# ScalarE issues the stores of its own results; the first batch is rotated at once, and the conversion of the first weights starts eight slots ahead of the first tile

## The chip, the cores and the metric

The kernel runs on one core of one Trainium2 chip. The metric is the device time of one execution in microseconds (us). Three timed runs of the kernel before gave 1304.89, 1307.54 and 1314.07 us; their median is 1307.54 us.

## What is computed

Three operators follow each other. Attention with rotated queries and keys (4 batches, 8 heads, 576 tokens, head size 64), then two layers of a feed-forward block over 2304 tokens of width 512 with an inner width of 2048. All inputs and outputs are float32 in the reference; the weights arrive as 64-bit floats.

```python
q_rot, k_rot = (rotate(q), rotate(k))       # x1*cos - x2*sin, x1*sin + x2*cos
scores = scale * np.matmul(q_rot, k_rot.transpose(0, 1, 3, 2))
attn = np.exp(scores - max); attn = attn / (sum + 1e-9)
x = np.matmul(attn, v)                      # then [B*S, H*D] = [2304, 512]
r = np.maximum(x @ w_in1, 0.0);  x = (s * r * r + b) @ w_out1
h = x @ w_in2;  out = (h / (1 + np.exp(-1.702 * h))) @ w_out2
```

## The kernel before, in words

**Attention.** The 8 heads of a batch are handled as 4 pairs. A *tile* is 128 query rows against 576 keys, and every tile has a number, its *slot*: 36 slots a batch, 144 in all. A pair has a first unit of 4 tiles (`k` = 0) and a second unit of 5; the first units of all four pairs come first (slots 0 to 15 of batch 0), then the second units. One tile is `score_tile` (TensorE makes `s`, VectorE takes the minimum and copies to `P`, ScalarE takes the exponential), `norm_tile` (GpSimd scales `P`), `turn_tile` (TensorE turns `P` into `t`, ScalarE and in the first 20 slots TensorE and ScalarE again split it into two float16 halves in `pt`), and at the end of a unit `weighted` (TensorE makes `av`, ScalarE scales it into `pt`, a store writes it to `xT` in DRAM).

**Rotation.** Before a pair can be scored, its q and its k are each loaded (`nat`), rotated by four elementwise instructions on GpSimd or VectorE (`rope_cross` twice, `rope_mul`, `rope_add`), turned by TensorE in two groups through one PSUM buffer (`r`), split by ScalarE and VectorE into two parts `z`, stored to DRAM (`ksp`, `qsp`) and loaded back (`k`, `qb`) by `fetch_pair`. In batch 0, VectorE rotates the q of pairs 0 and 1 (RV = 2) and GpSimd the other six. `plan_rope` starts pair p at slot -16 + 4p.

**Weights.** The 16 weight blocks `f` of each layer come in two *halves* (`m` = 0, 1) of 128x512. A half is loaded as 64-bit words (`stage`, 512 KB) and made into two float32 parts: one ScalarE scaling (L398), three VectorE instructions on the words (L399, L400, L403), one ScalarE copy (L406) and one GpSimd subtraction (L407). Layer 1's 32 halves are converted ahead of and among the tiles of batch 0: `CONV = (-12, 1.0)` puts block f at slot -12 + f. Eleven blocks are held in SBUF (`w0` to `w10`), five are written back to DRAM (`wd`) and streamed.

**Feed-forward layers.** `experts` makes *passes* over the tokens; a pass makes `l` (first product) and `acc` (second product) for all 16 blocks. From slot 22 of batch 0 on, its steps are put between the tiles. The first pass loads its `xl` from `xT` and thus needs the first units of all four pairs. After the last tile the passes run alone.

**Order of work.** The order on TensorE is pinned to the order in which the program is written. The other engines' queues are ordered by a scheduler from priorities (the slot) and its own estimate of when each instruction is ready. All DMAs are issued by SyncE in one queue (SP); each takes one of eight completion counters in turn (in the rows of order: DMAHW0 to DMAHW7) and waits first until the transfer that last used that counter has landed.

The lines printed here touch `rope_load`, `rope_cross` and `plan_rope` (rotation), `make_half` and `weight` (conversion), and `weighted` and `finish` (stores).

## Time and profile before

| what | value |
|---|---|
| median of three timed runs | 1307.54 us |
| the profiled execution, its own time | 1307.66 us |
| its span, first to last instruction | 1305.9 us |
| PE busy | 1119.6 us (86%) |
| DVE busy | 746.5 us (57%) |
| ACT busy | 676.7 us (52%) |
| POOL busy | 354.8 us (27%) |
| DMA | 202.5 MB, mean 155 GB/s |
| mean granted TensorE clock | 0.966 |

PE is TensorE, PEld its weight load, DVE VectorE, ACT ScalarE, POOL GpSimd, SP the queue of SyncE. Shares are averages over stretches with different limits: in its second half TensorE is busy nearly all the time, while in the first 200 us it is mostly idle and the other engines, the DMAs and the waits between them set the pace. So the profile is to be read by stretch.

### The profile page before, as it was taken

What the parts mean: (1) busy time and instruction counts of PE and PEld (TensorE: products, weight loads), DVE (VectorE), ACT (ScalarE), POOL (GpSimd) and SP (SyncE); (2) the same over time, 40 slices, a digit from 0 to 9 for tenths busy, and PEclk for the clock granted to TensorE, in tenths of its full rate; (3) what the DMA queues carried; (4) which work ended last, traced back from release to release, by engine and by line L of the source; (5) the groups of instructions that cost most, each with busy time, mean ns of one, the idle gap of its engine ahead of it and who ended that gap; (6) DMA issues with size and microseconds to landing.
All of it is one profiled execution on the core that took longest, in us unless ns stands there. A gap on an engine that the chain in (4) does not pass through costs nothing.

```text
span 1305.9 us, 21075 instructions
## 1 busy us (share of the span) xinstructions
PE 1119.6 (86%) x7432; PEld 991.4 (76%) x7432; DVE 746.5 (57%) x1652; ACT 676.7 (52%) x1483; POOL 354.8 (27%) x350
## 2 busy tenths in 40 slices
PE   0126568989989989999999996998999999999998
PEld 0024448988889888899889996876788888888887
DVE  7887735667657666757656657866633223232222
ACT  3347555666656666666656655665533223232232
POOL 5675743334324441444111112323100000000000
PEclk9998588999999999999999997999999999999999
DMA  7987765468756677665665528545303012021020
GB/s 241 307 272 243 243 173 149 139 196 252 224 155 211 197 230 228 191 212 169 187 195 172 166 73 289 166 148 170 117 17 113 1 49 81 17 74 24 17 81 17
DMA packets 131561, 202.50 MB, mean 155 GB/s; under 512 B 32512, under 2 KB 93440, under 8 KB 131456
## 3 DMA queue, kind: packets, MB, share of 16 engines
q1 hardware_dynamic: 131456, 201.15, 49.4%
q8 instruction: 59, 0.97, 0.3%
q14 instruction: 46, 0.38, 0.1%
HBM read 155.49 MB, written 45.61 MB: 154 GB/s over the span
## 4 chain that ended last, share of the span: by engine, by line
PE 56%; DMA 14%; DVE 9%; issue 8%; ACT 5%; POOL 4%; SPq 2%; DVEq 0%; POOLq 0%; ACTq 0%
PE acc L88 21%; PE l L88 21%; PE t L88 5%; PE s L88 4%; PE av L88 4%; DMA stage<-in_moe_w_in_dram 2%; DMA xT<-pt 2%; DVE P L299 2%; POOL w L407 2%; DMA xl<-xT 2%; DMA stage<-in_moe_w_out_dram 2%; DMA vr<-in_v_dram 1%; ACT P L308 1%; DVE stage L403 1%; DVE pt L342 1%
## 5 line engine op out<-in xcount | busy, mean ns | idle before, releaser
L88 PE MATMUL l<-xh,w 128*128 128x256 f32 (+1 forms) x1280 | 330.0, 331 | 11.9 <-ACT r L527 6.8
L88 PEld LDWEIGHTS l<-xh,w 128*128 128x128 f32 x1280 | 225.0, 191 | 36.0 <-ACT r L527 8.0
L88 PE MATMUL l<-xl,w 128*128 128x256 f32 (+1 forms) x640 | 211.8, 331 | 1.6 <-DVE xl L492 0.9
L319 POOL TENSOR_SCALAR P<-P,st 128x576 f32<-128x576 f32 x144 | 114.1, 793 | 345.3 <-DVE st L318 241.5
L88 PE MATMUL acc<-w,g 128*128 128x512 f32 x696 | 169.0, 392 | 4.9 <-ACT y L568 4.9
L308 ACT ACTIVATE P<-P,st 128x576 f32<-128x576 f32 x144 | 112.0, 778 | 101.8 <-DVE P L299 101.8
L532 DVE SCALAR_TENSOR_TENSOR r<-r,l 128x256 f32<-128x256 f32 x144 | 60.1, 417 | 180.2 <-ACT r L531 180.2
L88 PEld LDWEIGHTS acc<-w,g 128*128 128x128 f32 x696 | 131.1, 189 | 33.0 <-ACT y L568 5.8
L88 PE MATMUL t<-ident,P 128*128 128x128 f32 x720 | 111.7, 289 | 45.2 <-ACT pt L357 29.4
L531 ACT ACTIVATE r<-l 128x256 f32<-128x256 f32 x144 | 55.1, 383 | 178.9 <-PE l L88 178.8
L299 DVE TENSOR_SCALAR_CACHE_REDUCE P<-s 128x576 f32<-128x576 f32 x144 | 108.6, 754 | 62.9 <-PE s L88 57.4
L407 POOL TENSOR_TENSOR w<-stage,w 128x512 fp32r<-128x512 f32 x64 | 93.2, 1461 | 188.3 <-ACT w L406 146.2
L88 PEld LDWEIGHTS l<-xl,w 128*128 128x128 f32 x640 | 122.1, 191 | 13.3 <-DVE xl L492 2.0
L88 PEld LDWEIGHTS t<-ident,P 128*128 128x128 f32 x720 | 86.1, 148 | 58.7 <-issue 23.3
L88 PE MATMUL acc<-gh,w 128*128 128x256 f32 x616 | 129.4, 293 | 0.0
L88 PE MATMUL s<-k,qb 128*128 128x288 f32 x640 | 124.9, 324 | 3.9 <-DVE P L299 3.9
L342 DVE TENSOR_TENSOR pt<-t,pt 128x640 f16<-128x640 f32 x124 | 102.0, 822 | 28.3 <-ACT pt L340 27.6
L340 ACT CAST pt<-t 128x640 f16<-128x640 f32 x144 | 99.1, 688 | 21.2 <-PE t L88 19.4
L536 DVE TENSOR_TENSOR g<-r,g 128x256 fp32r<-128x256 f32 x160 | 71.0, 448 | 64.7 <-ACT g L535 64.7
L88 PEld LDWEIGHTS s<-k,qb 128*128 128x128 f32 x640 | 98.6, 204 | 12.2 <-issue 6.3
L529 ACT ACTIVATE r<-r,sb 128x256 f32<-128x256 f32 x144 | 86.1, 604 | 37.2 <-DVE r L528 36.7
L88 PEld LDWEIGHTS acc<-gh,w 128*128 128x128 f32 x616 | 102.6, 194 | 0.5 <-issue 0.4
(88 smaller groups left out, 1955.5 us busy)
## 6 DMA issues: line engine op xcount, KB each, us to landing
ws<-wd SPq DMA_DIRECT2D x96, 512.0 KB, 4.3
k<-ksp SPq DMA_DIRECT2D x32, 576.0 KB, 5.8
stage<-in_moe_w_in_dram SPq DMA_DIRECT2D x32, 512.0 KB, 5.0
stage<-in_moe_w_out_dram SPq DMA_DIRECT2D x32, 512.0 KB, 5.0
wd<-w SPq DMA_DIRECT2D x14, 512.0 KB, 5.0
ksp<-z SPq DMA_DIRECT2D x32, 160.0 KB, 5.0
qsp<-z SPq DMA_DIRECT2D x32, 160.0 KB, 4.4
vsp<-vz SPq DMA_DIRECT2D x16, 320.0 KB, 4.5
```

Source lines behind the costliest of these rows:

```text
L88: pin(nc.tensor.matmul(*args, **kw))
L299: nc.vector.tensor_scalar(pr.rearrange("p (n s) -> p n s", n=2), ps[:, :, :HS], -Q_SCALE, None, op0=ALU.mult, op1=ALU.min, accum_out=st[:, ...
L308: nc.scalar.activation(pr, pr, AF.Exp, bias=st[:, 0:1], scale=-1.0, accum_out=st[:, 1:2])
L319: nc.gpsimd.tensor_scalar(pr, pr, st[:, 2:3], 1.0, op0=ALU.mult, op1=ALU.mult)
L340: nc.scalar.copy(hi, pc)
L342: nc.vector.tensor_tensor(lo, pc, hi, op=ALU.subtract)
L403: nc.vector.scalar_tensor_tensor(low, high, 3, low, op0=ALU.logical_shift_left, op1=ALU.bitwise_or)
L407: nc.gpsimd.tensor_tensor(lo, f32(low), f32(hi), op=ALU.subtract)
L529: nc.scalar.activation(r, r, AF.Identity, bias=sb[:, 1:2], scale=sb[:, 0:1])
L531: nc.scalar.activation(r, ps[:, cols], AF.Tanh, scale=0.851)
L532: nc.vector.scalar_tensor_tensor(r, r, 1.0, ps[:, cols], op0=ALU.add, op1=ALU.mult)
L536: nc.vector.tensor_tensor(gl[:, cols], r, f32(gh[:, cols]), op=ALU.subtract)
```

## The change

Three things change. **Stores:** the stores of `xT`, of `x2` (between the layers) and of the output, 77 in all, are issued by ScalarE's queue instead of SP. **Rotation of batch 0:** loads and rotations of the four pairs start one slot apart (-16 + p instead of -16 + 4p), in buffers borrowed from weights `w5` to `w8` (`boot`), the turns are put at slots 4p - 7 and 4p - 8 and the ones after; VectorE also takes the q of pair 2 (RV = 3). **Conversion of layer 1:** block f is put at slot -8 + 1.5 f instead of -12 + f, its last two instructions (`split`, the ScalarE copy and the GpSimd subtraction) one slot later, and the raw words of blocks 0 to 12 go into the buffers of weights `w9` and `w10` instead of the ring of four that they shared with `xl`. `ACT_SHIFT` is empty, so that branch never runs.

```diff
+    boot = {}
+    BOOT = (5, 6, 7, 8)
 ...
     def rope_load(b, p, which, st):
-        nat = att.tile([128, RT, 2, HD], F32, tag="nat", name=f"nat{b}{p}{which}")
+        if b == 0:
+            if p not in boot:
+                boot[p] = wpool.tile([128, 2048], F32, tag=f"w{BOOT[p]}", name=f"boot{p}")
+            nat = boot_part(p, which)
+        else:
+            nat = att.tile([128, RT, 2, HD], F32, tag="nat", name=f"nat{b}{p}{which}")
 ...
     def weighted(g):
-        nc.sync.dma_start(
+        nc.scalar.dma_start(
             xT[128 * p : 128 * p + 128, b * S + q0 : b * S + q0 + T], xo[:, :T]
         )
 ...
     def make_half(t, w_in, w_out, f, m, nm):
+        elif f < HELD[0][-2]:
+            if m == 0:
+                stages[0] = wpool.tile(
+                    [128, 2, 512], U64, tag=f"w{len(HELD[0]) - 1 - f % 2}", name=f"stage{nm}"
+                )
+            raw = stages[0][:, m]
 ...
-        make_half(t, *W[layer], f, m, f"{layer}_{f}")
+        split = make_half(t, *W[layer], f, m, f"{layer}_{f}")
+        if layer == 0:
+            at(int(CONV[0] + CONV[1] * f) + WLAG, split)
+        else:
+            split()
 ...
     def finish(n, banks):
-                nc.sync.dma_start(
+                nc.scalar.dma_start(
                     x2[rows, t0 : t0 + T].rearrange("(c p) t -> p c t", p=128),
 ...
-                    nc.sync.dma_start(
+                    nc.scalar.dma_start(
                         ov[g // RT, ORDER_T[g % RT]], y[(j % 2) * 64 : (j % 2) * 64 + 64, j // 2]
 ...
-        gap = 2 if b else 1
         for g in range(2):
-            at(s + 4 + gap * g, rope_turn, b, p, which, g, st)
+            at(s + 4 + 2 * g if b else 4 * p + RT0 - which + g, rope_turn, b, p, which, g, st)
 ...
-    CONV = (-12, 1.0)
+    CONV = (-8, 1.5)
+    RT0 = -7
+    ACT_SHIFT = ()
+    WLAG = 1
-    RV = 2
+    RV = 3
 ...
-                eng = nc.vector if b == 0 and p < RV and which == 0 else nc.gpsimd
-                r = bounds[b - 1] + RS + 9 * p if b else -RL + 4 * p
+                eng = nc.vector if b == 0 and (p < RV and which == 0) else nc.gpsimd
+                r = bounds[b - 1] + RS + 9 * p if b else -RL + p
```

What this does to the queues is shown at three places. The first is GpSimd's queue from its first real work on, before the change (`rot` and `nat` are a rotation of the pair in the name's second digit, `w0_` the last step of a conversion, `vr` a memset in a value buffer).

```order
L195 TENSOR_TENSOR rot001_116<-nat001_112,tab_90 128x9x32 x2
L200 TENSOR_TENSOR nat001_112<-nat001_112,tab_90 128x576
L203 TENSOR_TENSOR nat001_112<-nat001_112,rot001_116 128x576
L407 TENSOR_TENSOR w0_0_128<-stage0_00_129,w0_0_128 128x512
L407 TENSOR_TENSOR w0_0_128<-stage0_01_137,w0_0_128 128x512
L407 TENSOR_TENSOR w0_1_158<-stage0_10_159,w0_1_158 128x512
```

The same place after the change (`boot0` to `boot3` are pairs 0 to 3, `nat101` is the k of batch 1).

```order
L208 TENSOR_TENSOR boot0_112<-boot0_112,tab_90 128x9x32 x2
L208 TENSOR_TENSOR boot1_115<-boot1_115,tab_90 128x9x32 x2
L213 TENSOR_TENSOR boot0_112<-boot0_112,tab_90 128x576
L213 TENSOR_TENSOR boot1_115<-boot1_115,tab_90 128x576
L208 TENSOR_TENSOR boot2_122<-boot2_122,tab_90 128x9x32 x2
L208 TENSOR_TENSOR boot3_134<-boot3_134,tab_90 128x9x32 x2
L216 TENSOR_TENSOR boot0_112<-boot0_112 128x576
L216 TENSOR_TENSOR boot1_115<-boot1_115 128x576
L208 TENSOR_TENSOR rot030_161<-boot3_134,tab_90 128x9x32 x2
L213 TENSOR_TENSOR boot2_122<-boot2_122,tab_90 128x576
L213 TENSOR_TENSOR boot3_134<-boot3_134,tab_90 128x576
L431 TENSOR_TENSOR w0_0_172<-stage0_0_173,w0_0_172 128x512
```

Pair 0's k was GpSimd's third instruction line and is now its seventh, behind half rotations of the three other pairs; the rotations of pairs 2 and 3 and of batch 1's first pair stand ahead of the first tile and not among the first sixteen any more.

The second place is VectorE's queue around the last part of q of pair 0 (`z000`), without which no tile can be scored; before the change:

```order
L403 SCALAR_TENSOR_TENSOR stage0_11_167<-stage0_11_167 128x512
L399 TENSOR_SCALAR stage0_20_200<-stage0_20_200 128x512
L217 TENSOR_TENSOR z000_188<-r0000_183,z000_188 128x2x256
L400 SCALAR_TENSOR_TENSOR stage0_20_200<-stage0_20_200 128x512
L403 SCALAR_TENSOR_TENSOR stage0_20_200<-stage0_20_200 128x512
L217 TENSOR_TENSOR z000_188<-r0001_219,z000_188 64x2x64
```

The same place after (`stage0_141` is the second half of block 14, `stage0_2` block 2, `vmx0` the maximum of a quarter of v, `vrow0` the scales made from it).

```order
L141 TENSOR_REDUCE vmx0_146<-vm0_3_170 128x1
L425 SCALAR_TENSOR_TENSOR stage0_141_1044<-stage0_141_1044 128x512
L149 TENSOR_REDUCE vm10_227<-vmx0_146 128x1
L151 TENSOR_REDUCE vrow0_225<-vps0_226 1x8
L159 TENSOR_SCALAR vrow0_225<-vrow0_225 1x8
L160 TENSOR_SCALAR vrow0_225<-vrow0_225 1x8
L421 TENSOR_SCALAR stage0_2_245<-stage0_2_245 128x512
L167 RECIPROCAL vrow0_225<-vrow0_225 1x8
L168 TENSOR_SCALAR vrow0_225<-vrow0_225 1x8
L169 TENSOR_SCALAR vrow0_225<-vrow0_225 1x8
L422 SCALAR_TENSOR_TENSOR stage0_2_245<-stage0_2_245 128x512
L230 TENSOR_TENSOR z000_210<-r0001_236,z000_210 64x2x64
```

That part of q now stands behind the conversion of blocks 0, 1, 13 and 14 (24 VectorE instructions, and two of block 2) and behind the scales of v; before, it stood behind 15 conversion instructions and no scales. Ahead of the first tile VectorE converts 10 halves (14 before); 20 follow between tiles 0 and 16 (18 before), the last two behind tile 16.

The third place is the first store of `xT`, after the change, in ScalarE's queue with the waits that each row has.

```order
L370 CAST pt010_688<-t5_731 128x5x128 [waits PE_49]
L417 ACTIVATE stage0_9_620<-stage0_9_620 128x512 [waits DMAHW1_49]
L391 DMA xT_104<-pt000_500 128x256 [waits DMAHW2_49,Activation_49]
L321 ACTIVATE P8_777,st8_776<-P8_777,st8_776 128x576 [waits DVE_49]
L430 CAST w0_9_619<-stage0_9_620 128x512 [waits DVE_49]
```

In SP's queue before the change it stood between a load of batch 1 and the next store.

```order
L394 DMA stage0_141_675<-in_moe_w_out_dram 128x512
L186 DMA nat101_943<-in_k_dram 128x576
L378 DMA xT_104<-pt000_684 128x256
L186 DMA nat100_973<-in_q_dram 128x576
L279 DMA vsp_108<-vz02_817 128x1280
```

The store has moved to an engine that computes, and its wait for a completion counter (DMAHW2, shared with SP's transfers) has moved with it. On TensorE, from the tenth tile on, every row stands in the same order as before.

## Rows read from the trace of the kernel before

**Rows 1.** Stretches: length, PE, PEld, DVE, ACT, POOL busy (count), clock, DMA share, GB/s

```profile
0.00:70.90 70.90, 11.33 (x38) 6.57 (x38) 58.16 (x84) 25.09 (x44) 42.79 (x39) 1.00 0.85 278
70.90:171.80 100.90, 52.90 (x271) 40.72 (x271) 77.07 (x136) 58.13 (x110) 64.36 (x54) 0.78 0.78 246
171.80:195.90 24.10, 13.34 (x105) 9.84 (x103) 10.03 (x35) 15.43 (x29) 13.03 (x14) 0.92 0.56 158
266.70:438.50 171.80, 157.51 (x1383) 150.05 (x1383) 115.18 (x283) 109.05 (x241) 64.61 (x72) 1.00 0.67 204
767.60:1305.90 538.30, 512.97 (x2421) 428.49 (x2419) 234.45 (x478) 216.42 (x507) 47.85 (x34) 0.98 0.27 86
```

**Rows 2.** The line of the tile's minimum: count, shortest/median/longest ns, first and last start

```profile
L299 DVE TENSOR_SCALAR_CACHE_REDUCE P<-s x144: 735/757/760, 70.9 to 767.6; 128x576 f32<-128x576 f32 x144
```

**Rows 3.** Chain that ended last, near the first pass: start, us, what

```profile
188.46 5.04 DMA xl<-xT
...
195.91 2.69 PE l L88 x11
```

**Rows 4.** VectorE's groups from 70.9 to 171.8 us: count, busy, mean ns, idle before

```profile
L400 DVE SCALAR_TENSOR_TENSOR stage<-stage 128x512 uint32<-128x512 uint32 x18 | 18.4, 1020 | 3.8 <-ACT stage L398 3.2
L403 DVE SCALAR_TENSOR_TENSOR stage<-stage 128x512 uint32<-128x512 uint32 x18 | 18.1, 1004 | 0.3
L399 DVE TENSOR_SCALAR stage<-stage 128x512 uint32<-128x512 uint32 x18 | 14.8, 824 | 0.0
L299 DVE TENSOR_SCALAR_CACHE_REDUCE P<-s 128x576 f32<-128x576 f32 x16 | 12.0, 753 | 10.1 <-PE s L88 8.8 <-POOL w L407 1.2
```

**Rows 5.** The three conversion lines over the whole run: shortest/median/longest ns

```profile
L399 DVE TENSOR_SCALAR stage<-stage x64: 408/430/1642, 11.5 to 931.9; 128x512 uint32<-128x512 uint32 x64
...
L400 DVE SCALAR_TENSOR_TENSOR stage<-stage x64: 672/693/1848, 13.7 to 932.6; 128x512 uint32<-128x512 uint32 x64
...
L403 DVE SCALAR_TENSOR_TENSOR stage<-stage x64: 669/692/1806, 14.7 to 933.3; 128x512 uint32<-128x512 uint32 x64
```

**Rows 6.** VectorE and GpSimd in order of time, the first rotations: start, us, instruction

```profile
7.57 1.82 POOL L195 TENSOR_TENSOR rot<-nat,tab 128x288 f32<-128x288 f32 x2 [6.27 <-DMA nat<-in_k_dram]
8.29 1.42 DVE L195 TENSOR_TENSOR rot<-nat,tab 128x288 f32<-128x288 f32 x2 [4.34 <-DMA nat<-in_q_dram]
9.47 1.50 POOL L200 TENSOR_TENSOR nat<-nat,tab 128x576 f32<-128x576 f32 x1
...
9.74 1.85 DVE L200 TENSOR_TENSOR nat<-nat,tab 128x576 f32<-128x576 f32 x1
...
11.05 1.79 POOL L203 TENSOR_TENSOR nat<-nat,rot 128x576 f32<-128x576 f32 x1
11.51 1.62 DVE L399 TENSOR_SCALAR stage<-stage 128x512 uint32<-128x512 uint32 x1
```

**Rows 7.** GpSimd's groups from 0 to 196 us: count, busy, mean ns, idle before

```profile
L407 POOL TENSOR_TENSOR w<-stage,w 128x512 fp32r<-128x512 f32 x32 | 46.6, 1459 | 25.1 <-ACT w L406 24.9
L195 POOL TENSOR_TENSOR rot<-nat,tab 128x288 f32<-128x288 f32 x20 | 21.0, 1072 | 12.2 <-DMA nat<-in_k_dram 11.7 <-DMA nat<-in_q_dram 0.6
...
L203 POOL TENSOR_TENSOR nat<-nat,rot 128x576 f32<-128x576 f32 x10 | 17.1, 1709 | 0.2
L200 POOL TENSOR_TENSOR nat<-nat,tab 128x576 f32<-128x576 f32 x10 | 15.8, 1581 | 0.2
```

**Rows 8.** DMA issues from 0 to 196 us: count, KB each, median us to landing

```profile
qsp<-z SPq DMA_DIRECT2D x10, 128.0 KB, 4.3
...
qb<-qsp SPq DMA_DIRECT2D x16, 64.0 KB, 4.3
```

**Rows 9.** The busiest stretch of the DMAs, columns as in rows 1

```profile
33.00:65.00 32.00, 5.78 (x19) 3.12 (x19) 28.09 (x41) 11.49 (x22) 21.36 (x16) 1.00 0.92 306
```

**Rows 10.** TensorE's largest wait for ScalarE from 196 to 784 us: us, times, longest

```profile
PE l L88 <- ACT r L527: 6.8, 5, 2.8
```

**Rows 11.** Stores on SP: issue of `xT` (shortest/median/longest ns)

```profile
L378 SPq DMA_DIRECT2D xT<-pt x32: 319/326/893, 127.9 to 782.5; - x32
```

**Rows 12.** The end of the run: start, us, what

```profile
1300.87 2.39 SPq L581 DMA_DIRECT2D out_dram<-y  x4
...
1300.93 0.60 ACT y L570
```

More of the change, by code (lines that the diff above doesn't have):

```diff
@@ L192, in rope_cross @@
     def rope_cross(b, p, which, st, eng):
-        rot = att.tile([128, RT, 2, HD], F32, tag="rot", name=f"rot{b}{p}{which}")
+        if b == 0 and which == 1:
+            rot = boot_part(p, 2)
+        else:
+            rot = att.tile([128, RT, 2, HD], F32, tag="rot", name=f"rot{b}{p}{which}")
         for e in range(2):
@@ L398, in make_half @@
         nc.scalar.activation(f32(high), f32(high), AF.Copy, scale=2.0**-112)
-        nc.vector.tensor_scalar(low, low, 29, None, op0=ALU.logical_shift_right)
+        if m in ACT_SHIFT and not late:
+            nc.scalar.activation(low, low, AF.Copy, scale=2.0**-29, bias=-0.5)
+        else:
+            nc.vector.tensor_scalar(low, low, 29, None, op0=ALU.logical_shift_right)
         nc.vector.scalar_tensor_tensor(
@@ L405, in make_half, with split @@
         )
-        nc.scalar.copy(hi, f32(low))
-        nc.gpsimd.tensor_tensor(lo, f32(low), f32(hi), op=ALU.subtract)
+        def split():
+            nc.scalar.copy(hi, f32(low))
+            nc.gpsimd.tensor_tensor(lo, f32(low), f32(hi), op=ALU.subtract)
+        return split
     W = ((w_in1, w_out1), (w_in2, w_out2))
@@ L424, in weight @@
             t = kept[layer][f][m]
-        make_half(t, *W[layer], f, m, f"{layer}_{f}")
+        split = make_half(t, *W[layer], f, m, f"{layer}_{f}")
+        if layer == 0:
+            at(int(CONV[0] + CONV[1] * f) + WLAG, split)
+        else:
+            split()
         if f in STREAMED[layer]:
@@ L459 @@
     late = {}
+    stages = {}
     def x_tile(nm, z=0):
```

2 lines of the change are left out of this document (added).

## The prediction

> **What bounds the kernel now.** Read first the table of stretches [rows 1], cut at four events: the first tile, the tile of slot 16, the start of the first pass, and the end of batch 0. TensorE is busy 92% of the time between 266.7 and 438.5 us and 95% after 767.6 us: there only TensorE's own work counts. Up to 195.9 us it is busy 77.6 us of 195.9, so the first 196 us are set by others, and the change works almost only there. The order on TensorE after it is unchanged, so I treat all from the first pass to the end as one block of 1305.9 - 195.9 = 1110 us that moves as a whole, and ask when the first pass starts.
>
> The first tile's minimum runs at 70.9 us [rows 2]; the first pass needs `xl`, which needs the stores of slots 0 to 15, and its products start at 195.9 us [rows 3]. So the head has three terms: A, to the first tile, 70.9 us; B, the sixteen tiles, 100.9 us; C, from there to the first pass, 24.1 us. In A and B VectorE is the busiest engine (58.2 of 70.9 and 77.1 of 100.9 us), the DMAs stand at 0.85 and 0.78 [rows 1]. VectorE's time is not all work: the three conversion instructions take 1020, 1004 and 824 ns in B [rows 4], and 672, 669 and 408 ns at their shortest [rows 5]. The rows in order of time show why [rows 6]: each VectorE instruction on SBUF data that runs beside GpSimd takes about as long as GpSimd's; four of the one pass while four of the other do.
>
> **Term A, to the first tile.** Gone from ahead of the first tile: four halves of conversion on VectorE. Added there: one rotation more on VectorE, and on GpSimd the rotations of k of pairs 2 and 3, q of pair 3 and batch 1's first pair. What the first tile needs last is the last part of q of pair 0, then its store, its reload and the value split. On VectorE that part stands behind 38 instructions that share data paths with GpSimd (12 of rotation, 26 of conversion).
>
> GpSimd's queue from 7.6 us [rows 6] to the end of pair 3's rotation is 12 half crosses, 5 products, 5 sums and 4 subtractions: 12 x 1.07 + 5 x 1.58 + 5 x 1.71 + 4 x 1.46 = 35.1 us [rows 7], and with batch 1's first product it ends at 7.6 + 36.7 = 44.3 us. It then waits for VectorE at the memsets of the value buffers, which need the last maxima. At one VectorE instruction for each of GpSimd's 27, VectorE is at its 27th shared one by then. Eleven are left to that part of q, about 11 x 0.6 = 6.6 us at the shortest durations [rows 5], plus some 5 us of maxima, scales and turns between them, in small instructions: 56 us. Store 4.3 us, reload 4.3 us [rows 8], some 4 us of issues in SP's queue between them (the value loads and the other reloads): 68 us. I take A = 68 us, 2.9 less than before. From below: with no sharing at all GpSimd's queue would still end near 43 us, and 12 us of store and reload follow, 55 us. From above: each of the 38 waits for the longest GpSimd instruction of rows 6, 1.82 us, 8.3 + 69 = 77, plus 14: 91 us.
>
> The Trainium skill, "SBUF — State Buffer", section "Who interferes with whom", says that GpSimd and a VectorE instruction with two SBUF inputs, or one in a two-port mode, lock each other out for a whole instruction. The trace agrees (1.85 us beside GpSimd's 1.50 and 1.79). The rule speaks against bunching the rotations: by it A would be 91 us if GpSimd always came first (the sum is then the third rival's below) and 55 us if the two never met (1280 us).
>
> **Term B, sixteen tiles.** VectorE's 77.1 us hold 51.3 us of conversions [rows 4], of which 18 x (0.672 + 0.669 + 0.408) = 31.5 us are work [rows 5], so 19.8 us are waiting for GpSimd, over GpSimd's 54 instructions: 0.37 us each. After the change GpSimd has 20 subtractions, 16 tiles and 2 memsets there, 38, since no rotation is left: 14 us of waiting. The two halves more cost 2 x 1.75 = 3.5 us, two splits of `z` 1 us. Busy: 77.1 - 19.8 + 14 + 3.5 + 1 = 75.8 us, almost what it was. The gain must come from VectorE's 23.8 idle us: 10.1 before the tiles' minima, 8.8 of them for TensorE [rows 4], which waits in its pinned order for turns whose rotations GpSimd has not finished. These go; the conversion's ScalarE copy, one slot later, also blocks ScalarE less. I leave 12 idle us: 88 us. From below, 76 us with VectorE never idle; from above 101, if the idle time stays.
>
> The DMAs allow it narrowly. Of the 19.7 MB that were moved ahead of the first tile (278 GB/s x 70.9 us) about 4 MB, mostly raw weights, come behind it now. B and C moved 24.8 + 3.8 = 28.6 MB [rows 1]; 32.6 MB at the best sustained rate, 306 GB/s [rows 9], take 107 us, and B + C of 88 + 25 leaves 113.
>
> **Term C.** The last two halves of conversion now stand behind slot 16. VectorE is busy only 10.0 of 24.1 us there [rows 1], so most of their 3.5 us lie beside other work: 25 us.
>
> **The stores.** 41 are of `xT` and `x2`, 36 of the output. On SP one takes 0.33 us (`xT`) to 0.60 us (output, 2.39 / 4) [rows 11, 12]; no row shows one on ScalarE, so I take the same. That is some 13 us of ScalarE's queue up to the second layer, where ScalarE is idle for 63 of 172 us [rows 1] and TensorE's largest wait for it is 6.8 us in 588 [rows 10]; and 22 us in the last layer, where it is busy 216 of 538. Both lie beside TensorE's work, I take 0 (bound 13 us, if the cover is gone). What SP gains is as little: it runs ahead of what needs its loads. At the very end it costs: SP issued the first output stores from 1300.87 us, while ScalarE still made the second half until 1301.53 [rows 12]; ScalarE can issue the four only after it. + 0.7 us.
>
> **The sum.** First pass at 68 + 88 + 25 = 181 us against 195.9: -14.9. With the end, -14.2. Against the profiled execution's own 1307.66 us (0.1 us over the median of 1307.54) that is 1293.4, rounded 1293 us, 1.1% less.
>
> **The rivals.** *The head runs better still.* If B falls to VectorE's 76 us and A to 62, the first pass starts at 163 us; the DMAs at 306 GB/s (48.3 MB) would need 158. 1307.7 - 32.9 + 0.7 = 1276 us. For it: VectorE's queue is then the only limit. Against it: the DMA share would have to stay above 0.9 for 100 us, and it was 0.78 in B [rows 1].
>
> *The DMAs or the idle time keep the head.* The 32.6 MB at B's own 246 GB/s take 132 us: first pass at 68 + 132 = 200, 1313 us. With B's idle time back (100 us) 193, 1306 us. For it: the share of 0.78 comes with SP's eight counters and its queue's waits, which stay.
>
> *The bunched rotations delay the first tile.* A = 91 us: first pass at 204, 1316 us. It decides against the change from A = 82 us on. Against it: GpSimd has to stop for VectorE at the memsets.
>
> *ScalarE waits for a completion counter.* Each `xT` and `x2` store now waits on ScalarE until the transfer that last used its counter has landed, with the exponential and the copies of the next tile behind it, and TensorE behind those. A landing takes about 4.3 us [rows 8]. If 1 us of it reaches TensorE in each of the 41, the gain turns: -14 + 41 = 1334 us; no gain is left at 0.35 us per store, and at 0.7 it is slower by over 1%. Against it: the counter's last user was placed eight DMAs earlier, so most of its landing is past when the store comes.
>
> **How the numbers follow.** A measurement of this kernel can tell about 1% (13 us) from no change. My forecast, 1286 to 1302 us, gets 0.49; the better head, below 1286, 0.20; the DMAs or the idle time, 1302 to 1313, 0.15; the late first tile 0.06; ScalarE's waits 0.10. Faster by over 1% (below 1294.5) is the better head and a little over half of the forecast, 0.47. Slower by over 1% is ScalarE's wait and the worst of the late tile, 0.12. The rest, 0.41, is within 1%. The range of 8 in 10 reaches from the better head's 1277 to 1315, beyond the DMA rival and up to the late tile. The likeliest one's own range is 1286 to 1302.
>
> **What would show it.** In the changed kernel's profile the first tile's minimum should start at about 68 us, the seventeenth at 156, the first pass at 181; VectorE should be busy about 76 us in B with fewer idle waits for TensorE, GpSimd without rotations there, DMA share about 0.9. From the first pass to the end it should be 1110 us. The forecast is wrong if that last stretch moves by more than some us (then the stores did it), if the first tile comes after 80 us, or if B keeps its 101 us with the DMA share unchanged.

## The result, and the profile after

The changed kernel is slower, by 0.8%: 1315.92 us (median of 10 runs, 1308.94 to 1320.55) against 1306.33 us of the kernel before (10 runs beside it, 1299.91 to 1314.07), a ratio of 1.0078, 95% interval 1.0054 to 1.0101. Forecast were 1293 us and 1.1% faster. The profiled execution took 1318.62 us, with a span of 1316.8.

The stretches of the changed kernel, cut at the same events as rows 1 (first tile, tile of slot 16, first pass), with the rest in two pieces; the columns are those of rows 1:

```profile
0.00:67.57 67.57, 8.30 (x30) 5.21 (x31) 54.35 (x73) 15.34 (x27) 47.96 (x42) 1.00 0.60 193
67.57:170.75 103.18, 54.94 (x281) 41.45 (x279) 71.48 (x151) 66.80 (x126) 49.44 (x44) 0.82 0.87 279
170.75:201.39 30.64, 18.75 (x102) 14.04 (x102) 11.08 (x39) 16.11 (x30) 15.19 (x17) 0.70 0.68 208
201.39:784.00 582.61, 537.41 (x4658) 513.87 (x4659) 370.90 (x928) 365.89 (x803) 187.16 (x211) 0.98 0.61 186
784.00:1316.80 532.80, 506.79 (x2365) 421.11 (x2363) 229.94 (x469) 211.89 (x498) 46.36 (x32) 0.98 0.27 86
```

| term | before [rows 1] | forecast | after |
|---|---|---|---|
| A, to the first tile | 70.9 | 68 | 67.6 |
| B, sixteen tiles | 100.9 | 88 | 103.2 |
| C, to the first pass | 24.1 | 25 | 30.6 |
| first pass starts at | 195.9 | 181 | 201.4 |
| from there to the end | 1110.0 | 1110 | 1115.4 |

Term A came out as forecast; B, and by less C, didn't. The same bytes were moved up to the first pass (length by GB/s: 13.0 + 28.8 + 6.4 = 48.2 MB after, 19.7 + 24.8 + 3.8 = 48.3 before), but 6.7 MB less of them ahead of the first tile. From 30 to 60 us the DMAs were busy for only a third of the time, as two stretches of A show (columns as above):

```profile
0.00:30.00 30.00, 1.12 (x4) 0.72 (x4) 21.90 (x26) 4.03 (x6) 21.53 (x23) 1.00 0.82 292
30.00:60.00 30.00, 3.88 (x14) 2.05 (x14) 28.75 (x39) 9.30 (x17) 21.97 (x17) 1.00 0.35 99
```

The kernel before had 0.92 and 306 GB/s from 33 to 65 us [rows 9]. Two views bear on it. In SyncE's DMA queue in order of time (start, us, what), the stores of the rotated rows and a value load hold up all that stands behind them; the waits of that queue up to the first tile (what it waited for: us in total, times, longest) name the releasers:

```profile
24.06 7.17 SPq L237 DMA_DIRECT2D ksp<-z  x2
31.49 3.79 SPq L236 DMA_DIRECT2D ksp<-z  x2
36.93 5.00 SPq L237 DMA_DIRECT2D qsp<-z  x2
42.03 0.55 SPq L413 DMA_DIRECT2D stage<-in_moe_w_out_dram  x1
42.62 0.44 SPq L408 DMA_DIRECT2D stage<-in_moe_w_in_dram  x1
50.73 0.66 SPq L271 DMA_DIRECT2D vr<-in_v_dram  x1
```

```profile
SPq L237 <- DVE z L230: 9.9, 2, 6.0
SPq L271 <- DVE stage L422: 8.2, 1, 8.2
```

Between 24 and 51 us that queue issues two loads of weights. And GpSimd, busy with rotations, does the last step of a block's conversion (L431 after, L407 before) only six times ahead of the first tile, against fourteen. These are its groups up to the first tile, first after, then before (count, busy, mean ns, idle before):

```profile
L431 POOL TENSOR_TENSOR w<-stage,w 128x512 fp32r<-128x512 f32 x6 | 9.2, 1547 | 4.9 <-ACT w L430 4.9
```

```profile
L407 POOL TENSOR_TENSOR w<-stage,w 128x512 fp32r<-128x512 f32 x14 | 19.9, 1418 | 19.9 <-ACT w L406 19.7
```

The raw blocks' buffers come free by that step. VectorE now converts 22 of the 32 half blocks among the sixteen tiles, against 18 before, and the last step of all starts at 171.59 us, before at 152.14. VectorE's groups in B, which answer to rows 4:

```profile
L425 DVE SCALAR_TENSOR_TENSOR stage<-stage 128x512 uint32<-128x512 uint32 x22 | 20.2, 918 | 0.3
L422 DVE SCALAR_TENSOR_TENSOR stage<-stage 128x512 uint32<-128x512 uint32 x22 | 17.3, 787 | 2.7 <-ACT stage L417 2.3
L312 DVE TENSOR_SCALAR_CACHE_REDUCE P<-s 128x576 f32<-128x576 f32 x17 | 12.8, 752 | 5.8 <-PE s L88 4.8 <-POOL P L332 0.9
L421 DVE TENSOR_SCALAR stage<-stage 128x512 uint32<-128x512 uint32 x22 | 11.3, 513 | 15.6 <-DMA stage<-in_moe_w_out_dram 12.1 <-DMA stage<-in_moe_w_in_dram 1.8 <-POOL w L431 1.6
```

A conversion step got shorter, as wanted (918, 787 and 513 ns against 1004, 1020 and 824), and VectorE's wait for TensorE fell from 8.8 to 4.8 us. But in front of the first step of a block (L421), where it never waited before, it now waits 15.6 us, 13.9 of them for weights on their way. The chain that ended last runs through these loads at the end of B (start, us, what):

```profile
145.31 0.53 SPq L242
...
145.89 0.43 SPq L252
...
146.42 6.93 DMA stage<-in_moe_w_out_dram
153.44 0.43 DVE stage L421
154.32 0.94 POOL P L332
155.41 2.76 POOL w L431 x2
...
160.18 6.29 DMA stage<-in_moe_w_out_dram
```

Ahead of the load at 146.42 us the chain is SyncE itself, which issues one DMA after another from 138 us on. In B it issues 128 DMAs and spends 77 of the 103 us on it; before, it was 116 DMAs and 63 of 101 us, with 81 DMAs ahead of the first tile against 58 now. By this trace the loads in B come late also because SyncE has to issue there what it didn't issue in A.

The stores, the other part of the change, cost what they cost before: an `xT` issue on ScalarE takes 326 ns in the median, as it did on SyncE [rows 11], and the four last output issues 2.43 us against 2.39 [rows 12] (of ScalarE's issues of `xT`: count, shortest/median/longest ns; then the end of the run):

```profile
L391 ACTq DMA_DIRECT2D xT<-pt x32: 326/326/362, 124.9 to 791.8; - x32
```

```profile
1311.03 1.28 ACT L601 ACTIVATE y<-acc 128x512 f32<-128x512 f32 x2 [2.09 <-PE acc L88]
1311.77 2.43 ACTq L612 DMA_DIRECT2D out_dram<-y  x4
```

### The profile page after: what moved, and what is told of

Its sections match the earlier page's. It is cut to its first block, busy times and chain, and to the rows that moved or that the text cites. A ratio compares the mean times of both kernels' runs of the same rounds, so it can differ in the third digit from the quotient of the medians.

```text
span 1316.8 us, 20989 instructions
## 1 busy us (share of the span) xinstructions
PE 1126.2 (86%) x7432; PEld 995.7 (76%) x7432; DVE 737.7 (56%) x1656; ACT 676.0 (51%) x1483; POOL 346.1 (26%) x346
## 4 chain that ended last, share of the span: by engine, by line
PE 55%; DMA 17%; DVE 11%; issue 7%; ACT 4%; SPq 3%; POOL 2%; ACTq 0%; DVEq 0%; POOLq 0%
PE l L88 21%; PE acc L88 21%; PE s L88 4%; PE av L88 4%; PE t L88 4%; DMA stage<-in_moe_w_in_dram 3%; DMA xl<-xT 3%; DMA xT<-pt 2%; DVE P L312 2%; DMA vm<-in_v_dram 2%; DMA stage<-in_moe_w_out_dram 2%; DVE pt L355 1%; POOL w L431 1%; DVE stage L422 1%; DMA ksp<-z 1%
## 5 line engine op out<-in xcount | busy, mean ns | idle before, releaser
L88 PE MATMUL l<-xh,w 128*128 128x256 f32 (+1 forms) x1280 | 331.8, 332 | 13.8 <-ACT r L558 8.0
L431 POOL TENSOR_TENSOR w<-stage,w 128x512 fp32r<-128x512 f32 x64 | 92.6, 1455 | 201.1 <-ACT w L430 166.4
L567 DVE TENSOR_TENSOR g<-r,g 128x256 fp32r<-128x256 f32 x160 | 70.8, 447 | 62.4 <-ACT g L566 62.3
```

Of the source, the lines that this page charges most:

```text
L88: pin(nc.tensor.matmul(*args, **kw))
L431: nc.gpsimd.tensor_tensor(lo, f32(low), f32(hi), op=ALU.subtract)
L567: nc.vector.tensor_tensor(gl[:, cols], r, f32(gh[:, cols]), op=ALU.subtract)
```

## The experiments

All ratios are to the kernel before, run beside them on the same chip, with 95% intervals, from 12 timed runs each (10 for the change itself, 7 for VectorE's rotations at once with the early conversion). Times of the head come from one profile each, and one profile alone is not worth much there, as the second profiles show. The letters in the expectations: S, the stores cost the time; D, the transfers that come behind the first tile; R, the bunched rotations; Q, SyncE's queue standing before the rotated rows' stores; M, the bytes among the tiles; K, dips of TensorE's clock behind the first pass; G, GpSimd busy with the bunch.

**How far one profile can be trusted.** The kernels after and before, unchanged, once more.

> The changed kernel once more, for a second profile of the same program: how much the first pass's start and the part behind it differ between two executions. Theory K (the scatter of the part behind the first pass comes from short dips of TensorE's clock, 1.7 us each, behind waits of 2 to 4 us, which are there in one execution and not in the next): first pass within 4 us of 201.4, the part behind it anywhere in 1110 to 1122, and longer by the dips that the profile shows between 220 and 780 us. If the order of the program sets the dips, they stand at the same four places as in the first profile (377, 391, 493, and 268 at the batch's start).

> The kernel before once more, for a second profile of the same program. Theory K: the part behind the first pass, 1110.0 in the first profile, in which only two dips of the clock stand between 220 and 780 us, is likely longer here (1110 to 1120), by about 3 us for each further dip; the first pass at 193 to 198 us. If the first profile was typical, 1109 to 1111 with two dips.

Measured: the changed kernel starts the first pass at 197.5 us (201.4 in the first profile) and then takes 1117.5 us (1115.4). The kernel before starts it at 189.4 us (195.9) and then takes 1114.0 (1110.0). So the profile that the prediction was worked from had a slow B (100.9 us; here 93.4) and a quick rest. In the mean of both pairs the head is 199.4 - 192.6 = 6.8 us longer after the change, and the rest about 4.4 us (1116.5 against 1112.0). By terms the head's 6.8 us are A -3.3, B +5.3 and C +4.8, so C carries nearly as much of the loss as B. Two profiles of one kernel differ by 3.9 and 6.5 us in the head and by 2.1 and 4.0 us in the rest, so neither is certain from profiles alone. Over the sixteen profiles of this study with all the work in them the rest lies between 1110.0 and 1122.3 us, with no order by edit; the first pass comes at 193.8 to 201.4 us in the eight profiles of kernels that are slower than before, and at 185.1 to 197.6 us in the other eight.

Part of the rest's scatter can be seen in TensorE's granted clock. Here is one place of the first profile after the change (columns as in the stretches): TensorE waits 2.78 us for ScalarE before its product at 376.15 us, and behind that the clock stands at 0.56 and 0.87 of full in two stretches of 3 us, that is for part of them at the lower of its two levels, 1.2 GHz, with TensorE busy all the time:

```profile
374.00:377.00 3.00, 0.85 (x7) 0.85 (x8) 1.91 (x5) 2.91 (x6) 0.02 (x1) 1.00 1.05 393
377.00:380.00 3.00, 3.00 (x16) 2.24 (x15) 2.20 (x7) 2.56 (x7) 0.73 (x1) 0.56 0.45 155
380.00:383.00 3.00, 3.00 (x23) 3.00 (x23) 1.98 (x10) 0.86 (x2) 0.75 (x1) 0.87 0.00 0
```

That costs (0.44 + 0.13) x 3 = 1.7 us. The kernel before has the same wait of 2.78 us in its first profile and keeps the full clock behind it:

```profile
368.00:371.00 3.00, 0.22 (x3) 0.07 (x1) 1.12 (x1) 2.20 (x5) 0.00 (x0) 1.00 1.01 395
371.00:374.00 3.00, 3.00 (x23) 2.60 (x24) 2.92 (x11) 2.81 (x7) 0.75 (x1) 1.00 0.73 233
```

In its second profile, where the wait is 2.60 us, the clock dips at that place. In the first one 8.1 us are lost in this way between 196 and 784 us (the stretch's length times what the clock lacks, summed over its microseconds), in the second 13.8; the two longest rests, 1121.3 and 1122.3 us, have 16.2 and 16.8. The dips don't explain all (one profile with 8.6 has a rest of 1117.3), and the expectation that they stand in the same places was half right: those at the second batch's start and at 486 to 497 us came again, those at 377 and 391 did not.

**The parts of the change, one at a time.** First only the stores, the three places of `xT`, `x2` and the output:

```diff
-        nc.sync.dma_start(
+        nc.scalar.dma_start(
```

> The kernel before with only the stores moved to ScalarE's queue (order of the head and all else as before). Theory S (the stores cost): from the first pass to the end it takes 1115 us, as in the changed kernel, and the whole 1312 us (ratio 1.004 to 1.005). Theory D (the head's transfers are the cause, the stores cost nothing outside it): first pass at 196 +- 2 us, 1110 +- 3 us from there, ratio 0.998 to 1.002.

Measured: 1.0012 (0.9983 to 1.0041), no change. The first pass starts at 192.7 us, and from there it takes 1115.8 us, as theory S had it; but that lies within the scatter above, and the ratio speaks against theory S. The Trainium skill, "DMA: Bandwidth & Descriptors", section "Issuing engines are not separate DMA queues", says that issuing from another engine saves only the issuing time; the ratio agrees.

Everything but the stores:

```diff
-        nc.scalar.dma_start(
+        nc.sync.dma_start(
```

> The changed kernel with the stores back in SP's queue. Theory S: 1110 us from the first pass to the end, first pass at 198 us, ratio to before about 1.001. Theory D: the head alone makes the loss: first pass at 199 to 202 us, 13 MB moved ahead of the first tile as in the changed kernel, ratio 1.004 to 1.008.

Measured: 1.0054 (1.0027 to 1.0082), first pass at 195.7 us (theory D wanted 199 to 202), 13.1 MB moved ahead of the first tile. So at least most of the loss is in the head's edits; the interval overlaps the whole change's. Of these edits, the later conversion alone (with its staging buffers and the last steps one slot later):

```diff
-    CONV = (-12, 1.0)
+    CONV = (-8, 1.5)
```

> Of the head, only the later conversion (block f at slot -8 + 1.5 f, staging in two weight buffers, the split one slot later); rotation, its buffers and RV as before, stores on SP. Theory D: fewer raw weights are moved ahead of the first tile (about 13 MB against 19.7), so the sixteen tiles stay bound by transfers: first tile at 55 to 65 us, sixteen tiles in 105 us or more, first pass at 195 to 205 us. A third theory, R (the bunched rotations are the cause): without them the later conversion gains, first pass before 190 us, ratio below 0.996.

Measured: 0.9986 (0.996 to 1.0012), no change, first pass at 193.1 us: neither theory's case. 18.3 MB were moved before the first tile, the sixteen tiles took 93.5 us. And the rotation at once alone, with the third pair's q on VectorE and the three-part buffers (borrowed here from `w7` to `w10`); the turns keep the slots that they had before the change (RT0 = -11), and the move of the turns by four slots was not tried by itself:

```diff
-                r = bounds[b - 1] + RS + 9 * p if b else -RL + 4 * p
+                r = bounds[b - 1] + RS + 9 * p if b else -RL + p
```

> Of the head, only the rotation at once (all four pairs from slot -16 + p, VectorE takes pair 2's q, buffers of weights w7 to w10); conversion from slot -12 at one slot per block and its ring as before, stores on SP. Theory D: about 17 MB or more are moved ahead of the first tile, the sixteen tiles take 85 to 95 us, first tile at 75 to 85 us, first pass at 188 to 196 us, ratio 0.994 to 1.000. Theory R: first tile after 85 us and the sixteen tiles not faster, first pass after 203 us, ratio above 1.005.

Measured: 1.007 (1.004 to 1.01), first pass at 197.0 us. So the rotation at once is enough by itself for about the whole loss. It is theory R's ratio, but not its way: the first tile comes at 70.8 us and not after 85.

Half of that pace, in the changed kernel:

```diff
-                r = bounds[b - 1] + RS + 9 * p if b else -RL + p
+                r = bounds[b - 1] + RS + 9 * p if b else -RL + 2 * p
```

> The changed kernel with the first batch's rotations two slots apart instead of one (four before). Theory R (the bunching itself costs): about half of the loss, 1310 to 1313, with the first tile's minimum at 67 to 71 us. Theory Q: the queue's standing time at the ksp and qsp stores, 16 us, falls to about half, and the stretch of sixteen tiles to 98 to 101 us. If the loss comes from something else in the early rotation (the three-part buffers, the third pair on VectorE), the whole stays at 1313 to 1319.

Measured: 1.0038 (1.0017 to 1.006) and 1311.9 us, where theory R wanted 1310 to 1313. That would be half of the loss, but the intervals touch (1.006 here, from 1.0054 on for the change). The stretch of sixteen tiles was 103.7 us and not shorter, so by its profile nothing shows where the half came back.

**Bytes, or what stands in the queue.** The weight spills among the tiles cut from 512 to 64 KB (their reloads read that part eight times, so the streamed blocks' values are not the right ones):

```diff
-                at(int(CONV[0] + CONV[1] * f) + SPILL, lambda: nc.sync.dma_start(d, f32(t)))
+                at(int(CONV[0] + CONV[1] * f) + SPILL, lambda: nc.sync.dma_start(d[:, 0, 0:128], f32(t)[:, 0, 0:128]))
 ...
-            nc.sync.dma_start(f32(w), spill[layer][f, m])
+            if layer:
+                nc.sync.dma_start(f32(w), spill[layer][f, m])
+            else:
+                src = spill[layer][f, m][:, 0, 0:128].unsqueeze(1).to_broadcast([128, 8, 128])
+                nc.sync.dma_start(f32(w).rearrange("p z (e c) -> p (z e) c", e=4), src)
```

> The changed kernel with the first layer's weight spills cut from 512 to 64 KB each (ten of them lie before the end of the sixteen tiles); the reloads read the same 64 KB eight times, so that weights of the first layer's streamed blocks are not the right ones. Left out are 8 x 448 KB = 3.6 MB in the stretch of sixteen tiles. Theory M (bytes hold the stretch): 3.6 MB at 279 GB/s is 13 us, so the stretch falls from 103 to 90 to 95 us. Theory Q and theory R: within 3 us of 103. The time of the whole says nothing, since the reloads change.

Measured, the stretch of sixteen tiles (columns as above):

```profile
67.58:173.83 106.25, 59.28 (x287) 43.97 (x285) 73.05 (x152) 68.57 (x128) 55.74 (x47) 0.58 0.80 247
```

It moved 26.2 MB (247 GB/s x 106.25 us) instead of 28.8, and took 3 us longer, where theory M wanted it shorter. That speaks against theory M, but it doesn't settle it: only 2.6 MB were left out of this stretch and not 3.6, TensorE's granted clock was 0.58 in it against 0.82, and this stretch differs by 7.4 us between the two profiles of the kernel before. Next, the stores of the rotated rows taken out of SyncE's queue:

```diff
-                nc.sync.dma_start(rows[:, :, 0:320], zz[0:64])
-                nc.sync.dma_start(rows[:, :, 320:S], zz[64:128, :, 0:256])
+                eng = nc.sync if b else nc.scalar
+                eng.dma_start(rows[:, :, 0:320], zz[0:64])
+                eng.dma_start(rows[:, :, 320:S], zz[64:128, :, 0:256])
```

> The changed kernel with one edit: the stores of the first batch's rotated rows (ksp, qsp; 32 of them) are issued by ScalarE, so SyncE's queue no longer stands before them (it did from 24 to 42 us in the changed kernel). Theory Q (what the rotation at once costs is SyncE's queue standing before these stores, so that loads come late and pile up behind the first tile): the bytes moved up to the first tile's minimum rise from 13.1 MB to at least 16, the stretch of sixteen tiles falls from 103 us to 97 or less, the whole to 1308 or less. Theory M (the stretch is held by the bytes that it moves, 28.8 MB at 279 GB/s, wherever they are issued): bytes and stretch within 5% of the changed kernel's, the whole 1313 to 1319. Theory K (the loss sits behind the first pass, in dips of TensorE's granted clock): the stretch may fall, the whole stays at 1312 to 1319.

Measured: 1.0039 (1.0019 to 1.0059) and 1311.1 us, between what theory Q and theory M wanted, though the interval still touches the change's; first tile at 70.2 us, B 98.0 us, first pass at 196.9. But only 14.7 MB were moved before the first tile, not 16: the queue now stands elsewhere, and one of the new waits is for GpSimd's last conversion step (its waits up to 75 us; us in total, times, longest):

```profile
SPq L272 <- DVE stage L426: 12.9, 1, 12.9
SPq L414 <- POOL w L432: 9.6, 1, 9.6
```

The same edit on top of the later conversion alone, where the rotations keep their old pace:

> The later conversion alone (the first batch rotated at the pace of the kernel before, all other stores on SyncE), with the stores of the first batch's rotated rows issued by ScalarE. Theory Q: SyncE's queue stands little in this order (11 us before 16.6 us, little behind), so no more than 2 us better than the later conversion alone: 1303 to 1307, the stretch of sixteen tiles 90 to 95 us. Theory M: as the later conversion alone, 1305 to 1307. If ScalarE's waits at these stores delay the first pieces of work behind them, 1309 or more.

Measured: 1.0019 (0.9996 to 1.0041), 1310.0 us, B 96.3 us: no gain where the queue didn't stand. It is the case in which ScalarE's waits were to cost something, but the interval overlaps that of the later conversion alone, so this isn't shown.

**GpSimd taken out.** All eight rotations of the first batch on VectorE; first in the kernel before, at its pace, then at once with the conversion as early as before (otherwise the kernel with the rotation alone):

```diff
-                eng = nc.vector if b == 0 and p < RV and which == 0 else nc.gpsimd
+                eng = nc.vector if b == 0 else nc.gpsimd
```

> The kernel before with all eight rotations of the first batch on VectorE (two of them before). Theory G together with what the slow conversions beside GpSimd's rotations suggest (1.0 us against 0.68 alone): GpSimd loses six rotations of about 5.5 us, VectorE gains six of 2.3 us, and the 96 conversion steps fall from 989 ns to about 800; the first pass starts 3 to 8 us earlier than at 195.9, the whole is 1300 to 1305. If the head is held by the transfers (19.7 MB before the first tile at a share of 0.85), nothing moves: 1305 to 1309. If VectorE is the bound of the head, 1309 to 1314.

> All rotations of the first batch on VectorE and at once, with the conversion as early as in the kernel before and all stores on SyncE: against the run with the paced rotations on VectorE (1301.0) only the pace differs, against the one at once with the later conversion (1312.6) only the conversion and ScalarE's stores. If the pace is the cause even without GpSimd (four pairs' rotations stand in front of the first tile and push weights' loads behind it), 1309 to 1314, with 16 MB or less moved before the first tile. If the later conversion is, 1300 to 1304.

Measured: paced 0.9951 (0.9926 to 0.9977), 1301.0 us, as theory G had it; at once 0.9949 (0.9925 to 0.9973), 1299.9 us. With the early conversion, then, the pace costs nothing when VectorE rotates, and 0.7% when GpSimd does. The two kernels with the rotation at once and the early conversion differ in nothing but the engine of five rotations. Their first two stretches, first with GpSimd, then with VectorE:

```profile
0.00:70.82 70.82, 11.34 (x40) 6.86 (x41) 54.35 (x73) 17.68 (x32) 48.91 (x45) 1.00 0.66 209
70.82:170.84 100.02, 52.80 (x270) 39.95 (x269) 81.86 (x151) 65.00 (x123) 48.83 (x43) 0.63 0.92 290
```

```profile
0.00:64.69 64.69, 11.54 (x40) 7.04 (x41) 56.28 (x96) 19.85 (x35) 27.67 (x26) 1.00 0.78 245
64.69:160.33 95.64, 52.25 (x271) 39.20 (x269) 74.26 (x150) 63.94 (x120) 49.00 (x43) 0.66 0.92 291
```

GpSimd is busy 27.7 us before the first tile instead of 48.9, VectorE only 1.9 us longer although it does five rotations more, and the first pass starts at 185.1 instead of 197.0 us. The paced kernel starts it at 187.0. Both beat the kernel before and the change. For the run at once 1309 to 1314 or 1300 to 1304 us were expected; 1299.9 is at the lower edge of the second, the case that lays the loss of the next run on the later conversion or on what goes with it.

VectorE's rows ahead of the first tile show why it is busy only 1.9 us longer. Three rotations beside GpSimd's five took 6.6 + 5.0 + 3.9 = 15.5 us; all eight took 3.3 + 3.2 + 6.0 + 4.1 + 3.0 = 19.6 us, that is 2.5 us each instead of 5.2. First with GpSimd, then with VectorE:

```profile
L208 DVE TENSOR_TENSOR rot<-boot,tab 128x288 f32<-128x288 f32 x6 | 6.6, 1144 | 5.0 <-DMA boot<-in_q_dram 5.0
L213 DVE TENSOR_TENSOR boot<-boot,tab 128x576 f32<-128x576 f32 x3 | 5.0, 1707 | 0.0
L216 DVE TENSOR_TENSOR boot<-boot,rot 128x576 f32<-128x576 f32 x3 | 3.9, 1337 | 0.0
```

```profile
L213 DVE TENSOR_TENSOR boot<-boot,tab 128x576 f32<-128x576 f32 x8 | 6.0, 748 | 0.0
L216 DVE TENSOR_TENSOR boot<-boot,rot 128x576 f32<-128x576 f32 x4 | 4.1, 1021 | 0.0
L208 DVE TENSOR_TENSOR rot<-boot,tab 128x288 f32<-128x288 f32 x8 | 3.3, 448 | 0.0
L208 DVE TENSOR_TENSOR boot<-boot,tab 128x288 f32<-128x288 f32 x8 | 3.2, 452 | 3.5 <-DMA boot<-in_k_dram 3.5
L216 DVE TENSOR_TENSOR boot<-boot 128x576 f32<-128x576 f32 x4 | 3.0, 747 | 0.0
```

Among the sixteen tiles both kernels move their bytes at the same rate (290 and 291 GB/s, share 0.92), near the best rate before, 306 GB/s [rows 9]. The 1.2 MB by which the second moves less there are 4 us at that rate, and the stretch is 4.4 us shorter. So here the DMAs' rate may be what holds the tiles, and theory M isn't out.

The wait for weights' loads, 13.9 us in the changed kernel, isn't the way in which the rotation alone costs its 0.7%: with GpSimd, in the same stretch, VectorE waits 1.3 us for them.

```profile
L421 DVE TENSOR_SCALAR stage<-stage 128x512 uint32<-128x512 uint32 x22 | 11.3, 512 | 1.4 <-DMA stage<-in_moe_w_in_dram 0.7 <-DMA stage<-in_moe_w_out_dram 0.6
```

The same edit in the changed kernel, alone and together with the stores of the rotated rows on ScalarE:

> The changed kernel with all eight rotations of the first batch on VectorE (three of them before, five on GpSimd). Theory G (the rotations in a bunch keep GpSimd busy for 48 of the first 67.6 us, so that the conversions' last step, GpSimd's, comes six times before the first tile instead of fourteen, the blocks' buffers come free late and the weights' loads move behind the first tile): five rotations of about 8 us leave GpSimd, VectorE takes five times 2.3 us, at least ten of the last steps lie before the first tile, the sixteen tiles take 95 us or less instead of 103, the whole is 1309 or less. Theory Q (SyncE's queue before the rotated rows' stores alone): GpSimd's share doesn't matter, the stretch stays at 98 to 104, the whole at 1311 to 1317. If VectorE becomes what the head waits for, the first tile comes at 72 us or later and the whole at 1314 or more.

> The changed kernel with two edits at once that each took back about half of its loss: all rotations of the first batch on VectorE, and the stores of the rotated rows issued by ScalarE. If GpSimd's bunch and SyncE's queue are two causes that add up, both halves go: 1306 to 1309, no slower than the kernel before. If they are two ends of one wait (the rotated rows come late, and whatever stands behind them), the second edit adds nothing: 1311 to 1314. In both cases the sixteen tiles keep 60 or more of the 96 conversion steps, since the later start of the conversions is still in.

Measured: 1.0039 (1.0011 to 1.0067) and 1.006 (1.0041 to 1.0079); first pass at 193.8 and 193.9 us. Less than theory G wanted was won by moving GpSimd's rotations (eight last steps before the first tile for ten, B 99.5 us for 95, 1312.6 us for 1309). Both intervals overlap the change's, so a gain from either edit isn't clear of the noise, and the second adds none: they are not two causes that add up. In the second kernel VectorE waits 0.5 us among the tiles for weights' loads, and it is no quicker for that:

```profile
L422 DVE TENSOR_SCALAR stage<-stage 128x512 uint32<-128x512 uint32 x20 | 11.1, 556 | 0.5 <-DMA stage<-in_moe_w_in_dram 0.5
```

What is left, 1.0039 against the 0.9949 of the run at once, must lie in what else differs: the later conversion with its staging buffers and later last steps, ScalarE's stores, and two things that the expectation of the run at once passed over, the turns four slots later (RT0 = -7 for -11) and the rotations' buffers (`w5` to `w8` for `w7` to `w10`). By itself the later conversion does no harm, neither with GpSimd's rotations (0.9986 above) nor with VectorE's:

> All rotations of the first batch on VectorE at the pace of the kernel before (1301.0 by itself), with the later conversion (1306.2 by itself, no change). If what holds the head is the work that stands ahead of the first tile on VectorE and GpSimd, fewer conversions there add to it: the first tile's minimum at 60 to 62 us, the first pass at 183 to 187, the whole 1298 to 1301. If each conversion moved behind the first tile costs as much there as it frees ahead of it, 1300 to 1303. If the tiles' stretch now waits for weights' loads (as after the change), 1303 to 1308.

Measured: 0.997 (0.995 to 0.9989), 1301.7 us, the middle case; first tile at 67.8 us and not at 60 to 62, first pass at 187.1.

| rotations of the first batch | conversion early | conversion later |
|---|---|---|
| mostly GpSimd, paced | 1 (before) | 0.9986 |
| mostly GpSimd, at once | 1.007 | 1.0054; 1.0078 with ScalarE's stores |
| VectorE, paced | 0.9951 | 0.997 |
| VectorE, at once | 0.9949 | 1.0039 with ScalarE's stores |

In the column on the right the rotation at once loses about 0.7% with either engine (0.9986 to 1.0054, 0.997 to 1.0039), on the left only with GpSimd. All kernels at once on the right also have the turns four slots later, and in all others the turns keep their slots. So in the changed kernel the loss is not laid on GpSimd by these runs; the late turns, the rotations' buffers, and the later conversion or ScalarE's stores together with the pace are rivals that no run takes apart.

## Why the prediction was wrong, point by point

**Term A, right in size.** 67.6 us for 68. The two ends, 55 and 91 us, were never near. The last part of q of pair 0 starts at 56.56 us, for the 56 of the text, and GpSimd's bunch, batch 1's first product included, ends at 45.16 + 1.85 = 47.0 us for 44.3. So the way was right too.

**Term B, the step that failed.** The text left VectorE 12 idle us of 88. VectorE's busy time came out close (71.5 us for 75.8) and the wait for TensorE did go down, but the idle time was 103.2 - 71.5 = 31.7 us (29.3 in the second profile), with 13.9 us of waiting for weights' loads that no row of before showed. With 103.2 us for 88, B is the term that missed most. The step that failed is this one: that VectorE's idle time falls from 23.8 to 12 us because the waits for TensorE go, with nothing in their place. Beside it, "about 4 MB come behind the first tile" was too low: 6.7 MB came (19.7 - 13.0), and the sum then asked only whether the DMAs could move them at their best rate, 306 GB/s. In the trace SyncE's queue stands before the rotated rows' stores in A, and in B the loads have to wait their turn behind its other issues. Whether the rate held them as well is open: the run with the cut spills speaks against it, the stretches at a share of 0.92 speak for it. And what the wait for loads costs is not shown, since the rotation alone loses as much with 1.3 us of it, and the paced kernel on VectorE, quicker than the kernel before, has 12.0 us of it up to its first pass (8.2 + 3.8, below). The baseline was high too: the second profile of the kernel before has 93.4 us for the 100.9 that the sum started from. The price of emptying GpSimd's queue in B was taken from B's rows, and what GpSimd's full queue in A does to the blocks behind it was left out: the sum took four halves of conversion away from ahead of the first tile, and eight of GpSimd's last steps went.

**Term C.** 30.6 us for 25 (28.1 in the second profile). The text put VectorE's last two halves into C. They ran in B (22 halves there by VectorE's rows, for the 20 of the text's sum), and of the conversion only GpSimd's last step, at 171.59 us, stands behind the seventeenth tile's minimum. VectorE was busy 11.1 us there for 10.0 before. What grew is TensorE's busy time, 18.75 us for 13.34 with 102 products for 105, at a granted clock of 0.70 against 0.92: 5.4 of the 6.5 us by which C is longer (16.79 us at 0.74 in the second profile). The sum had taken no account of the clock. Why it was lower there stays open.

**The rest.** 1110 us were taken from one profile. They were the shortest of all, and equal kernels differ by 2 to 4 us in it. The 4.4 us by which the rest is longer in the mean of two profiles each can't be told from that. Together with the head's 6.8 us they make 11.2, for 9.6 measured.

**The stores.** Taken as 0: the run with the stores alone shows 0.1%, and by its interval no more than 0.4%. The rival of ScalarE waiting for a completion counter, which needed 0.35 us a store, is excluded by the same run. The 0.7 us at the end didn't come: from the last output's result to the span's end it is 4.5 us after and 4.4 before.

**The rivals.** The one that came was "the DMAs or the idle time keep the head", first pass at 200 us and 1313 us: measured 201.4 and 197.5, and 1315.9. It had a chance of 0.15, and its price was near by luck: it had 32.6 MB behind the first tile at 246 GB/s and a share of 0.78, and 28.8 + 6.4 = 35.2 MB came at 263 GB/s, with a share of 0.87 in B. The bunched rotations were a rival too, but with the wrong victim: the first tile was in time. The rule of the Trainium skill, "SBUF — State Buffer", section "Who interferes with whom", cited there for A (GpSimd and VectorE lock each other out of a shared pair of ports), bears on what took its place: with the rotations of the kernel before on VectorE alone, the 96 conversion steps up to the first pass take (28.9 + 26.1 + 21.9) / 96 = 801 ns instead of 989 (34.3 + 34.0 + 26.6 us), and VectorE's busy time up to the first pass falls from 145.3 [rows 1] to 139.5 us, though it does six rotations more (143.2 us in the second profile of the kernel before). That one engine locks the other out isn't shown by this, only that their work is longer side by side. These are VectorE's groups up to 185 us in that paced kernel:

```profile
L400 DVE SCALAR_TENSOR_TENSOR stage<-stage 128x512 uint32<-128x512 uint32 x32 | 28.9, 907 | 2.2 <-ACT stage L398 1.1 <-DVE stage L399 0.5
L403 DVE SCALAR_TENSOR_TENSOR stage<-stage 128x512 uint32<-128x512 uint32 x32 | 26.1, 819 | 0.3
L399 DVE TENSOR_SCALAR stage<-stage 128x512 uint32<-128x512 uint32 x32 | 21.9, 688 | 12.2 <-DMA stage<-in_moe_w_out_dram 8.2 <-DMA stage<-in_moe_w_in_dram 3.8
```

**What is shown and what isn't.** Shown: the rotation at once by itself brings about the whole loss, the stores and the later conversion by themselves bring none; and with the early conversion it does so only with GpSimd rotating (only the engine changed: 1.007 to 0.9949). Not shown: that GpSimd is the cause in the changed kernel, where VectorE's rotations at once still lose 0.4 to 0.6%. Argued from one trace only, and against other traces: the way by which the bunch costs the time, blocks freed late and loaded late. A rival for it is that the rotations and conversions themselves take longer on VectorE beside GpSimd (5.2 for 2.5 us a rotation); no run tells the two apart. The number of last steps ahead of the first tile alone doesn't measure it: nine in the slow kernel with the rotation alone, ten in the quick one with VectorE. Open: what makes the rotation at once lose on VectorE with the later conversion, why TensorE's clock was lower in C, and how much of the rest's 4.4 us is real.

## What to carry to other kernels

When work is pulled ahead of a milestone on an engine that others need for short steps, ask what stands behind it in that engine's queue, which buffers these steps free, and what the work costs the engine beside it. A load can be late while the DMAs are two thirds idle, so an amount of bytes over the best rate is only a lower bound. A wait that stands out in one trace is not yet a cause: here quick kernels had it too, and a slow one lacked it. And before a sum rests on a stretch of one profile, take a second profile, since here equal programs differed by 6.5 us in the head, as much as the change itself.

## What the runs showed of the hardware

Rotations on VectorE took about twice as long with GpSimd's rotations beside them: three took 15.5 us beside five on GpSimd, and all eight 19.6 us when only batch 1's first pair was left to GpSimd. So moving five from GpSimd to VectorE made VectorE's busy time before the first tile only 1.9 us longer (54.35 to 56.28 us) and GpSimd's 21.2 us shorter (48.91 to 27.67). A wait of TensorE of 2.78 us was followed by a fall of its granted clock to the lower level, 1.2 GHz, in one execution, which cost 1.7 us beside the wait, and by none in another, of a kernel with the same wait.
